# Fusing Phi into K's weights with products of 64 and 60 rows in place of products of 120 rows

## The chip, the core and the metric

The kernel runs on one core of one Trainium2 chip. The metric is the device time of one execution in microseconds (us), the median of several. TensorE (PE in the views) multiplies; its weight loads (PEld) are instructions of their own. VectorE (DVE), ScalarE (ACT) and GpSimd (POOL) do the rest of the arithmetic, and SyncE (SP) issues all the DMAs.

## What is computed

`x` has 2048 tokens of 640 values. It is normalized by row, goes through linear attention with 32 heads of 20 values (A) and beside it through a gated unit of width 1536 (B), and the two results are added to `x`.

```python
def _A_ref(x, wqkv, w_phi, wo):
    B, S, D = x.shape
    H = 32; Dh = D // H
    qkv = (lambda x, *d: x.transpose(*d))((x @ wqkv).reshape(B, S, 3, H, Dh), 2, 0, 3, 1, 4)
    q, k, v = qkv[0], qkv[1], qkv[2]
    pq = jnp.einsum("bhsd,hdf->bhsf", q, w_phi)
    pk = jnp.einsum("bhsd,hdf->bhsf", k, w_phi)
    phi_q = jnp.concatenate([_softmax(pq, axis=-1), _softmax(-pq, axis=-1)], axis=-1)
    phi_k = jnp.concatenate([_softmax(pk, axis=-1), _softmax(-pk, axis=-1)], axis=-1)
    kv = jnp.einsum("bhsf,bhsd->bhfd", phi_k, v)
    z  = jnp.einsum("bhsf->bhf", phi_k)
    num = jnp.einsum("bhqf,bhfd->bhqd", phi_q, kv)
    den = jnp.einsum("bhqf,bhf->bhq", phi_q, z)[..., None] + 1e-6
    o = num / den
    return (lambda x, *d: x.transpose(*d))(o, 0, 2, 1, 3).reshape(B, S, D) @ wo
...
def _B_ref(x, w1, w3, w2):
    gate = jnp.einsum("bsd,df->bsf", x, w1)
    up = jnp.einsum("bsd,df->bsf", x, w3)
    h = _silu(gate) * up
    out = jnp.einsum("bsf,fd->bsd", h, w2)
...
return x + _A_ref(xn, A_wqkv, A_w_phi, A_wo) + _B_ref(xn, B_w1, B_w3, B_w2)
```

Since `pk = xn Wk Phi`, with Phi block-diagonal (a 20x20 block for each head), the kernel forms the 640x640 matrices `Wk Phi` and `Wq Phi` once. This document is about how these small products are made.

## The kernel before

The order of every engine's work is written out by hand (`tc.manual_schedule`, line 156): each engine runs its instructions in the order of the Python text, and semaphores do the rest. SP's queue has the DMAs in that order too.

**The start** (lines 173 to 235 and 756 to 823). The first tiles of `x`, 128 tokens each, and the weights for V are loaded. Until `x` is there, TensorE is given idle products: two of ones (line 225) and 40 products 64 columns wide on a tile of zeros, `warm(2 * WARM, P // 2)` (line 226). Then come the transposes of the first tiles by TensorE (`by_pe`, line 294), whose PSUM results ACT copies (line 301), and the norm's statistics (`ln_stats`, `ln_root`). A one-element copy on POOL (line 775) makes the DMA of `x` tiles 4 and 5 wait for the root of tile 1; the first slices of the gated unit's weights w1 and w3 (`ld_glu1`) stand around it in SP's queue. `warm(4)` (line 759) stands between the first two groups of transposes.

**Fusing Phi.** `ldT` (line 157) loads Wk, and later Wq, transposed by the DMA: slice `c` has 128 columns of the weight from column `AT[c]` on in its 128 partitions. `AT` is 0, 120, ... 480 and 520, so a slice's first 120 rows hold six heads of 20. `wps` holds the rows of `w_phi` that belong to them, and POOL spreads them with a mask of ones and zeros into blocks (`phi_blocks`, line 431): `wphi[:, c]` is a 120x120 block-diagonal piece of Phi. `fuse` (line 437) makes one 128-row piece `d` (of five) of the fused matrix with six products, `c` = 0 to 5, of 120 contraction rows: the transposed weight is the stationary operand (128 columns of it, reloaded for each product) and `wphi[:, c]` moves, 120 columns wide, 40 for the last. Slices 0 to 2 land in one PSUM bank (360 columns), 3 to 5 in another (280). ACT copies the first to `wkphi` or `wqphi`, DVE or ACT the second.

K's five pieces, `FB(0)` to `FB(4)` (line 747), stand at lines 885 to 894: FB(0) and FB(1) together, FB(2) and FB(3) together, FB(4) alone; V's product of a token tile (`V(14)`, and that for tile 15) stands between them. Right behind FB(4) comes the loop over the 16 token tiles (line 901), whose `phi_unit` multiplies a tile by `wkphi` (five row pieces, two products each) and takes the exponentials. Q's five pieces are made inside this loop, in its turns 4 to 8 (line 908), for the loop over Q's tiles behind it. Other small products in the trace: `kv_unit` (line 498, products 61 columns wide) and `r_unit` (line 530, 63 wide).

Of the kernel before, what the change touches and what calls it, by code (L numbers as in the profile page):

```python
# [8 lines left out]
P = 128  # L9
# [3 lines left out]
def kernel(  # L13
# [17 lines left out]
    nc = tc.nc  # L31
    bf = mybir.dt.bfloat16
# [10 lines left out]
    EPS = 1e-5  # L43
    SAFE = 36.0
    BY_ROOT = 6
    WARM = 20
    RAW = 3


# [2 lines left out]
    CH = 6 * 3 * Dh  # L52

    VC = 1 + 3 * Dh

    NF, FR, LH = 6, 120, 6
    AT = [120 * c for c in range(5)] + [D - 120]

    x2 = A_x[0]
    out2 = out[0]  # L60
# [1 line left out]
    one = ctx.enter_context(tc.tile_pool(name="one", bufs=1))  # L62
# [4 lines left out]
    def bank(name, dt=f32):  # L67
        n = 512 if dt == f32 else 1024
        return psum.tile([P, n], dt, name=name, tag="bank")

    def pair(name):
        return psum2.tile([P, 2, 512], f32, name=name, tag="pair")


    xnT = one.tile([P, KD, S], bf, name="xnT")
    wkphi = one.tile([P, KD, D], bf, name="wkphi")
    wqphi = one.tile([P, KD, D], bf, name="wqphi")
    w1 = one.tile([P, KD, F], bf, name="w1")
    w3 = one.tile([P, KD, F], bf, name="w3")
    kvr = one.tile([P, NCH, 3, 21], bf, name="kvr")  # L80
# [64 lines left out]
    def ld(dst, src):  # L145
        nc.sync.dma_start(out=dst, in_=src)
# [4 lines left out]
    def ld_glu(f0, f1):  # L151
        for w, src in ((w1, B_w1), (w3, B_w3)):
            ld(w[:, :, f0:f1], src[:, f0:f1].rearrange("(c p) f -> p c f", p=P))

    wps = one.tile([P, NF, Dh], bf, name="wps")
    with tc.manual_schedule():
        def ldT(dst, i, c):
            a = i * D + AT[c]
            nc.sync.dma_start_transpose(out=dst[:, c], in_=A_wqkv[:, a : a + P])
# [19 lines left out]
        for c in range(2, KD):  # L179
# [7 lines left out]
        eps = one.tile([P, 1], f32, name="eps")  # L187
        nc.gpsimd.memset(eps[:], EPS)

        mask = one.tile([P, LH], bf, name="mask")  # L190
        nc.gpsimd.memset(mask[:], 1.0)
        nc.gpsimd.affine_select(
            out=mask[:], in_=mask[:], pattern=[[-20, LH]], base=0,
            channel_multiplier=1, compare_op=ALU.is_ge, fill=0.0,
        )
        nc.gpsimd.affine_select(
            out=mask[:], in_=mask[:], pattern=[[20, LH]], base=19,
            channel_multiplier=-1, compare_op=ALU.is_ge, fill=0.0,
        )

# [4 lines left out]
            out=own[:], in_=own[:], pattern=[[-64, 2], [-20, 3]], base=0,  # L205
# [3 lines left out]
            out=own[:], in_=own[:], pattern=[[64, 2], [20, 3]], base=19,  # L209
# [5 lines left out]
        idle = bank("idle")  # L215
        nought = one.tile([P, P], bf, name="nought")
        nc.vector.memset(nought[:], 0.0)

        def warm(n, cols=P):
            for _ in range(n):  # L220
                nc.tensor.matmul(idle[:, 0:cols], nought[:], nought[:, 0:cols])  # L221

        lit = nc.const_aps.tensor(1.0, [P, P], bf)
        for _ in range(2):
            nc.tensor.matmul(idle[:, 0:P], lit, lit)
        warm(2 * WARM, P // 2)

        nc.gpsimd.memset(phi[:, :, :, :, 60:64], 0.0)

# [11 lines left out]
        def ln_stats(*ts):  # L241
            made = []
            for t in ts:
                xt = xin[:, (t // 4) % 3, t % 4, :]
                st = work.tile([P, 2, 6], f32, name="st")
                for i in range(2):
                    nc.vector.bn_stats(out=st[:, i, :], in_=xt[:, i * HD : (i + 1) * HD])  # L247
                made.append(st)
            for t, st in zip(ts, made):
                nc.vector.bn_aggr(out=mv[:, t, :], in_=st[:])  # L250
# [43 lines left out]
        def by_pe(dst, t, ps):  # L294
            xt = xin[:, (t // 4) % 3, t % 4, :]
            for c in range(KD):
                nc.tensor.transpose(
                    ps[:, c * P : (c + 1) * P], xt[:, c * P : (c + 1) * P], ident[:]
                )
# [48 lines left out]
        def tile_of(t):  # L348
            return slice(t * P, (t + 1) * P)

        def by_token(cols, w, name, cut, ps=None):

            ps = ps or [bank(name), bank(name)]
            for c in range(KD):
                for i in range(2):
                    a, b = (0, cut) if i == 0 else (cut, D)
                    nc.tensor.matmul(  # L357
                        ps[i][:, 0 : b - a],
                        xnT[:, c, cols],
                        w[:, c, a:b],  # L360
                        start=(c == 0),
                        stop=(c == KD - 1),
                        skip_group_check=True,
                    )
            return ps
# [63 lines left out]
        wphi = one.tile([P, NF, LH, Dh], bf, name="wphi")  # L429

        def phi_blocks():
            nc.gpsimd.tensor_mul(
                out=wphi[0:FR],
                in0=wps[0:FR, :, None, :].to_broadcast([FR, NF, LH, Dh]),
                in1=mask[0:FR, None, :, None].to_broadcast([FR, NF, LH, Dh]),
            )

        def fuse(dst, wT, d, ps, copy=None):

            for c in range(NF):  # L440
                b, i = divmod(c, 3)
                h0 = 4 if c == NF - 1 else 0
                nc.tensor.matmul(  # L443
                    ps[b][:, FR * i : FR * i + Dh * (LH - h0)],
                    wT[0:FR, c, d * P : (d + 1) * P],
                    wphi[0:FR, c, h0:LH],
                    start=(i == 0),
                    stop=(i == 2),
                    skip_group_check=True,
                )  # L450
            nc.scalar.copy(out=dst[:, d, 0:CH], in_=ps[0][:, 0:CH])
            (copy or nc.scalar.copy)(out=dst[:, d, CH:D], in_=ps[1][:, 0 : D - CH])

        def glu_unit(sc, fi, banks=None):

# [243 lines left out]
        def fill(n):  # L699
            for _ in range(n):  # L700
                glu_unit(*glu.pop(0))()
# [38 lines left out]
        def two(name):  # L740
            both = pair(name)
            return both[:, 0], both[:, 1]

        def V(t, ps=None):
            v_unit(vaug[:, t], tile_of(t), ps)

        def FB(d):
            fuse(wkphi, wkT, d, [bank("pf"), bank("pf")] if d % 2 else two("pf"), nc.scalar.copy if d == 4 else nc.vector.tensor_copy)


        def by_dma(t):
# [4 lines left out]

        pst = [bank("pst", bf), bank("pst", bf)]
        by_pe(xrT, 0, pst[0])
        warm(4)
        ln_stats(0)  # L760
        ln_root(0)
        by_pe(xrT, 1, pst[1])
# [71 lines left out]
        ld_tiles(12, 2)  # L834
        ld_tiles(14, 2)
        w_phi = A_w_phi.rearrange("h j f -> (h j) f")
        ld(wps[0:FR, 0:5], w_phi[0 : 5 * FR].rearrange("(c p) f -> p c f", p=FR))
        ld(wps[0:FR, 5], w_phi[D - FR : D])
        stats(8, 2)
        g3 = unit()  # L840
        g2()
# [40 lines left out]
        V(13)  # L882
        g8 = unit()
        g8()
        FB(0)
        FB(1)
        ld_glu(512, F)
        V(14)
        FB(2)
        FB(3)  # L890
        for c in range(NF):
            ldT(wqT, 0, c)
        ps = by_token(tile_of(15), wv, "pv", CH)
# [7 lines left out]
        for i, t in enumerate(turns):  # L901
            phi_unit(t, wkphi, "pk")
            if i > 1:
                kv_unit(turns[i - 2], vaug[:, turns[i - 2]], acc, i == 2, False)
            if i and i not in (2, 3, 6, 7, 14, 15):
                fill(1)
            if 4 <= i < 9:
                fuse(wqphi, wqT, i - 4, [bank("pf"), bank("pf")])
            fill(1)
            if i == 0:  # L910
                nc.sync.dma_start_transpose(out=wvT, in_=A_wqkv[:, 2 * D : 3 * D])
            if 4 <= i < 9:
                column_sum(i - 4)
            if i == 9:
                ld(row[:].rearrange("c p -> p c"), sums[:])
                ld(less_sum, row[:].rearrange("c p -> (c p)").partition_broadcast(P))
            if 11 <= i < 11 + RAW:
                raw_centred(i - 11)
            if i >= 12:
                norm_unit(wkphi, 0, i - 12)  # L920
# [71 lines left out]
    with tc.If(ok == 0) as general:  # L992
# [4 lines left out]
        with tc.For_i(0, NST, 1) as t:  # L997
            cols = bass.ds(t * P, P)
# [4 lines left out]
            for i, half in enumerate(halves):  # L1003
                n = half.shape[1]
                nc.vector.tensor_tensor(out=half, in0=half, in1=acc[:, i, 0:n], op=ALU.add)
        kv_done(halves)
        with tc.For_i(0, NST, 1) as t:
# [5 lines left out]
            h = hT[:, bass.ds(t, 1)].rearrange("p a f s -> p (a f) s")  # L1013
# [33 lines left out]
```

## Time and profile before

| what | value |
|---|---|
| median of 3 runs | 267.82 us (267.74 to 268.05) |
| the profiled execution: its own time | 269.46 us |
| the profiled execution: span from the first to the last instruction | 267.7 us |
| busy share of the span | PE 97%, DVE 72%, PEld 57%, ACT 43%, POOL 34% |

The profile is of one execution. Its views give for each instruction the engine, the line of the kernel, the tile written, the tiles read (`out<-in`), and start and duration. A matmul's row has the array's rows and columns in use (`120*128`) and the operand's shape (partitions x columns). A matmul's duration runs from its start to a modelled end, and matmuls overlap: the pace of a row of matmuls is read from their number and the time from the first start to the next group's start, which the chain of waits gives. A few matmul records are missing from a trace.

### The profile page before, as it was taken

Reading aid. Unit: us, or ns where it says so; the run is one execution under the profiler, and the core shown is the slowest. Engines: PE = TensorE matmul, PEld = TensorE weight load, DVE = VectorE, ACT = ScalarE, POOL = GpSimd, SP = SyncE. Lnnn points to the kernel's source line nnn. Section 1 sums busy time; section 2 is a strip of 40 time slices with the busy share of each in tenths; the row PEclk is TensorE's granted clock in tenths of the full one; section 3 lists DMA queues with packets and bytes.
Section 4 is the critical chain, followed back from the end, with each engine's and each line's share of the span. In section 5 each row is a group of like instructions: output and inputs, shape, how many; then the busy total and the mean of one; then the engine's idle time right before and its main releaser. Section 6 shows DMA issues by size and latency. Waiting matters only on the chain.

```text
span 267.7 us, 5000 instructions
## 1 busy us (share of the span) xinstructions
PE 260.8 (97%) x1840; PEld 152.9 (57%) x1866; DVE 192.9 (72%) x355; ACT 113.8 (43%) x349; POOL 90.7 (34%) x83
## 2 busy tenths in 40 slices
PE   8979999999999999999999999999999999999995
PEld 7756565756556555555555555555555554644573
DVE  5879982488877777799988999999799876215121
ACT  5863445664567754455856664432422240000000
POOL 5022540035544633444364333335533553000000
PEclk9999999999999999999999999999999999999999
DMA  6994966996000000700007945363964979553681
GB/s 194 285 177 114 152 126 124 385 146 125 1 0 2 1 3 2 172 2 0 2 0 196 210 107 120 85 157 85 125 145 111 180 183 176 127 122 66 177 226 55
DMA packets 82828, 31.25 MB, mean 117 GB/s; under 512 B 71279, under 2 KB 81391, under 8 KB 82800
## 3 DMA queue, kind: packets, MB, share of 16 engines
q1 hardware_dynamic: 82800, 30.89, 53.0%
q8 instruction: 16, 0.26, 0.4%
q14 instruction: 12, 0.10, 0.1%
HBM read 11.17 MB, written 2.63 MB: 52 GB/s over the span
## 4 chain that ended last, share of the span: by engine, by line
PE 94%; DMA 3%; issue 1%; ACT 1%; DVE 0%; SPq 0%; POOL 0%
PE up L459 18%; PE gp L459 18%; PE acc L645 15%; PE pq L357 8%; PE pk L357 8%; PE acc L598 7%; PE pv L357 6%; PE acc L650 6%; DMA w<-in_B_w_dram 3%; PE pr L535 2%; PE pkv L500 2%; PE pf L443 1%; PE up L476 1%; PE idle L221 1%; ACT reg_w L301 0%
## 5 line engine op out<-in xcount | busy, mean ns | idle before, releaser
L423 POOL TENSOR_TENSOR phi<-phi,rk 128x1320 bf16<-128x1320 bf16 x32 | 77.2, 2414 | 109.3 <-DVE rk L422 87.7
L459 PEld LDWEIGHTS <-w 128*128 128x128 bf16 x450 | 42.6, 97 | 46.9
L420 DVE TENSOR_REDUCE sk<-phi 128x66 f32<-128x1320 bf16 x32 | 48.8, 1525 | 19.7 <-ACT phi L386 18.4
L459 PE MATMUL up<-xnT,w 128*128 128x512 bf16 x224 | 55.9, 379 | 0.2
L459 PE MATMUL gp<-xnT,w 128*128 128x512 bf16 x207 | 54.4, 378 | 0.8
L357 PEld LDWEIGHTS <-xnT 128*128 128x128 bf16 x450 | 42.8, 98 | 19.2
L386 ACT ACTIVATE phi<-pq 128x360 bf16<-128x360 f32 (+2 forms) x96 | 24.8, 366 | 42.1 <-issue 31.8
L470 ACT ACTIVATE th<-gp 128x512 f32<-128x512 f32 x48 | 29.4, 612 | 28.1 <-PE gp L459 26.8
L645 PE MATMUL acc<-reg_h,reg_v 128*128 128x512 bf16 x180 | 41.3, 379 | 0.0
L490 DVE SCALAR_TENSOR_TENSOR reg_h<-gs,up 128x512 bf16<-128x512 bf16 x48 | 33.0, 687 | 5.4 <-PE pv L357 0.5
L487 DVE SCALAR_TENSOR_TENSOR gs<-th,gp 128x512 bf16<-128x512 f32 x48 | 31.4, 653 | 5.2 <-ACT th L470 5.2
L386 ACT ACTIVATE phi<-pk 128x360 bf16<-128x360 f32 (+2 forms) x96 | 24.9, 370 | 19.4 <-PE pk L357 19.4
L645 PEld LDWEIGHTS <-reg_v 128*128 128x128 bf16 x180 | 17.4, 98 | 19.1
L357 PE MATMUL pk<-wkphi,xnT 128*128 128x360 bf16 (+1 forms) x160 | 24.3, 299 | 0.0
L357 PE MATMUL pq<-wqphi,xnT 128*128 128x360 bf16 (+1 forms) x160 | 24.3, 299 | 0.0
L422 DVE RECIPROCAL rk<-sk 128x66 f32<-128x66 f32 x32 | 18.1, 567 | 3.2
L357 PE MATMUL pv<-reg_w,xnT 128*128 128x360 bf16 (+1 forms) x130 | 18.6, 299 | 0.0
L247 DVE BATCH_NORM_STATS2 st<-reg_h 128x6 f32<-128x320 bf16 x32 | 13.4, 476 | 3.5 <-DMA reg_h<-in_A_x_dram 3.5
L653 DVE TENSOR_TENSOR w<-acc,v_raw 128x512 bf16<-128x512 f32 x10 | 6.6, 670 | 11.6 <-issue 5.8
L607 DVE TENSOR_TENSOR res<-acc,xr 128x320 bf16<-128x320 f32 (+2 forms) x8 | 3.6, 487 | 15.7 <-PE acc L598 10.8
L372 ACT CAST reg_v<-pv 128x360 bf16<-128x360 f32 (+2 forms) x39 | 10.6, 347 | 9.7 <-PE pv L357 9.7
L556 DVE TENSOR_TENSOR o__77<-pr,den 128x360 bf16<-128x360 f32 (+1 forms) x32 | 14.2, 485 | 0.6
(90 smaller groups left out, 210.7 us busy)
## 6 DMA issues: line engine op xcount, KB each, us to landing
w<-in_B_w_dram SPq DMA_DIRECT2D x2, 1280.0 KB, 7.2
reg_v<-in_B_w_dram SPq DMA_DIRECT2D x1, 1920.0 KB, 8.8
out_dram<-w SPq DMA_DIRECT2D x6, 320.0 KB, 2.7
reg_h<-in_A_x_dram SPq DMA_DIRECT2D x5, 320.0 KB, 5.6
w<-in_B_w_dram SPq DMA_DIRECT2D x4, 320.0 KB, 9.3
reg_h<-in_A_x_dram SPq DMA_DIRECT2D x6, 160.0 KB, 2.9
reg_w<-in_A_wqkv_dram SPq DMA_DIRECT2D x5, 160.0 KB, 3.7
reg_w<-in_A_wo_dram SPq DMA_DIRECT2D x1, 800.0 KB, 7.3
```

The source lines that it names most:

```text
L357: nc.tensor.matmul(ps[i][:, 0 : b - a], xnT[:, c, cols], w[:, c, a:b], start=(c == 0), stop=(c == KD - 1), skip_group_check=True,)
L386: nc.scalar.activation(out=dst[:, c0 : c0 + n, g, 0:k], in_=p.rearrange("p (c f) -> p c f", c=n), func=AF.Exp, scale=1.0 - 2.0 * g,)
L420: nc.vector.reduce_sum(out=sk[:], in_=rows, axis=AX.X)
L422: nc.vector.reciprocal(out=rk[:], in_=sk[:])
L423: nc.gpsimd.tensor_mul(out=rows, in0=rows, in1=rk[:, :, :, None].to_broadcast([P, 2 * NCH, 3, Dh]))
L459: nc.tensor.matmul(ps, w[:, c, fi * P : (fi + 1) * P], xnT[:, c, sc * 512 : (sc + 1) * 512], start=(c == 0), stop=(c == KD - 1),)
L470: nc.scalar.activation(out=th[:], in_=gp, func=AF.Tanh, scale=0.5)
L487: nc.vector.scalar_tensor_tensor(out=gs[:], in0=th[:], scalar=1.0, in1=gp, op0=ALU.add, op1=ALU.mult)
L490: nc.vector.scalar_tensor_tensor(out=hT[:, 4 * sc : 4 * sc + 4, fi, :], in0=gs[:].rearrange("p (t s) -> p t s", t=4), scalar=0.5, in1=up.r ...
L598: nc.tensor.matmul(ps[:, 0 : b - a], rows[j][0], rows[j][1][:, a:b], start=(j == 0), stop=(j == len(rows) - 1),)
L645: nc.tensor.matmul(acc4, w2[:, k, cols], hT[:, 4 * g : 4 * g + 4, k, :], start=(k == 0), stop=False,)
L650: nc.tensor.matmul(acc[:], wo[:, k, cols], oTs[g][:, k, :], start=False, stop=(k == KD - 1),)
```

## The change

Three things change together.

1. K's fusion. `AT` becomes 0, 36, 156, ... 516, and a slice's first 124 rows are used. Slice 0 gives heads 0 and 1 in one product over 124 rows, 60 columns wide (20 columns of zeros ahead of the two heads; `wkphi` has 20 columns more in front for them). Each further slice holds six heads in rows 4 to 123: three in rows 4 to 63 and three in rows 64 to 123. Two products are made of it, one over rows 0 to 63 into one PSUM bank and one over rows 64 to 123 into the other, each 60 columns wide. FB(0) and FB(1) are merged, and FB(2) and FB(3): the 124-row products of both pieces come first, then the pairs. ACT's copy takes the six groups of 60 of one bank to every other group of the result, the other copy the five groups of the other bank.
2. Q's fusion keeps one product for a slice, now over 124 rows: 60 columns for the first and 120 for the five others. POOL's spreading of Phi and the load of `wps` are split differently (slice 0, slices 1 to 5).
3. The 40 idle products 64 columns wide become 8 that are 256 wide (64 columns, each read four times) and 8 that are 64 wide.

```diff
-    NF, FR, LH = 6, 120, 6
-    AT = [120 * c for c in range(5)] + [D - 120]
+    NF, FR, LH = 6, 124, 6
+    AT = [0] + [2 * Dh - 4 + LH * Dh * c for c in range(NF - 1)]
...
-    wkphi = one.tile([P, KD, D], bf, name="wkphi")
-    wqphi = one.tile([P, KD, D], bf, name="wqphi")
+    wkpad = one.tile([P, KD, Dh + D], bf, name="wkphi")
+    wqpad = one.tile([P, KD, Dh + D], bf, name="wqphi")
+    wkphi, wqphi = wkpad[:, :, Dh:], wqpad[:, :, Dh:]
...
-        def warm(n, cols=P):
+        def warm(n, cols, times=1):
             for _ in range(n):
-                nc.tensor.matmul(idle[:, 0:cols], nought[:], nought[:, 0:cols])
+                nc.tensor.matmul(
+                    idle[:, 0 : cols * times], nought[:],
+                    nought[:, 0:cols, None].to_broadcast([P, cols, times]),
+                )
...
-        warm(2 * WARM, P // 2)
+        warm(8, P // 2, 4)
+        warm(8, P // 2)
...
+        def fuse_rows(dst, wT, parts):
+
+            def product(d, ps, c, b, r0, r1, h):
+                i = c - b
+                nc.tensor.matmul(
+                    ps[b][:, 60 * i : 60 * i + 60],
+                    wT[r0:r1, c, d * P : (d + 1) * P],
+                    wphi[r0:r1, c, h : h + 3],
+                    start=(i == 0),
+                    stop=(c == NF - 1),
+                    skip_group_check=True,
+                )
+
+            for d, ps, _ in parts:
+                product(d, ps, 0, 0, 0, FR, 0)
+            for d, ps, copy in parts:
+                for c in range(1, NF):
+                    product(d, ps, c, 1, 0, 64, 0)
+                    product(d, ps, c, 0, 64, FR, 3)
+                groups = dst[:, d].rearrange("p (c k) -> p c k", k=60)
+                for b, n, op in ((0, 6, nc.scalar.copy), (1, 5, copy)):
+                    op(
+                        out=groups[:, b::2],
+                        in_=ps[b][:, 0 : 60 * n].rearrange("p (c k) -> p c k", k=60),
+                    )
...
-                h0 = 4 if c == NF - 1 else 0
+                a = 120 * i - (60 if 0 < c < 3 else 0)
                 nc.tensor.matmul(
-                    ps[b][:, FR * i : FR * i + Dh * (LH - h0)],
+                    ps[b][:, a : a + (120 if c else 60)],
                     wT[0:FR, c, d * P : (d + 1) * P],
-                    wphi[0:FR, c, h0:LH],
+                    wphi[0:FR, c, 0 : 6 if c else 3],
...
-        warm(4)
+        warm(4, P)
...
-        FB(0)
-        FB(1)
+        FB(0, 1)
         ld_glu(512, F)
         V(14)
-        FB(2)
-        FB(3)
+        FB(2, 3)
```

More of the change, by code (lines that the diff above doesn't have):

```diff
@@ L45 @@
     BY_ROOT = 6
-    WARM = 20
     RAW = 3
@@ L188 @@
         nc.gpsimd.memset(eps[:], EPS)
-        mask = one.tile([P, LH], bf, name="mask")
+        mask = one.tile([P, 2, LH], bf, name="mask")
         nc.gpsimd.memset(mask[:], 1.0)
         nc.gpsimd.affine_select(
-            out=mask[:], in_=mask[:], pattern=[[-20, LH]], base=0,
+            out=mask[:], in_=mask[:], pattern=[[-24, 2], [-20, LH]], base=20,
             channel_multiplier=1, compare_op=ALU.is_ge, fill=0.0,
@@ L196 @@
         nc.gpsimd.affine_select(
-            out=mask[:], in_=mask[:], pattern=[[20, LH]], base=19,
+            out=mask[:], in_=mask[:], pattern=[[24, 2], [20, LH]], base=-1,
             channel_multiplier=-1, compare_op=ALU.is_ge, fill=0.0,
@@ L431, in phi_blocks, with fuse @@
         def phi_blocks():
[L432 to L438, printed above, removed]
+            for k, a, b in ((0, 0, 1), (1, 1, NF)):
+                nc.gpsimd.tensor_mul(
+                    out=wphi[0:FR, a:b],
+                    in0=wps[0:FR, a:b, None, :].to_broadcast([FR, b - a, LH, Dh]),
+                    in1=mask[0:FR, k : k + 1, :, None].to_broadcast([FR, b - a, LH, Dh]),
+                )
[21 more added lines that the diff above has]
+                        in_=ps[b][:, 0 : 60 * n].rearrange("p (c k) -> p c k", k=60),
+                    )
+        def fuse(dst, wT, d, ps):
             for c in range(NF):
                 b, i = divmod(c, 3)
-                h0 = 4 if c == NF - 1 else 0
+                a = 120 * i - (60 if 0 < c < 3 else 0)
                 nc.tensor.matmul(
-                    ps[b][:, FR * i : FR * i + Dh * (LH - h0)],
+                    ps[b][:, a : a + (120 if c else 60)],
                     wT[0:FR, c, d * P : (d + 1) * P],
-                    wphi[0:FR, c, h0:LH],
+                    wphi[0:FR, c, 0 : 6 if c else 3],
                     start=(i == 0),
@@ L450, in fuse @@
                 )
-            nc.scalar.copy(out=dst[:, d, 0:CH], in_=ps[0][:, 0:CH])
-            (copy or nc.scalar.copy)(out=dst[:, d, CH:D], in_=ps[1][:, 0 : D - CH])
+            nc.scalar.copy(out=dst[:, d, 0:300], in_=ps[0][:, 0:300])
+            nc.scalar.copy(out=dst[:, d, 300:], in_=ps[1][:, 0:360])
         def glu_unit(sc, fi, banks=None):
@@ L745, in V, with FB @@
             v_unit(vaug[:, t], tile_of(t), ps)
-        def FB(d):
-            fuse(wkphi, wkT, d, [bank("pf"), bank("pf")] if d % 2 else two("pf"), nc.scalar.copy if d == 4 else nc.vector.tensor_copy)
+        def FB(*ds):
+            fuse_rows(wkpad, wkT, [
+                (d, [bank("pf"), bank("pf")] if d % 2 else two("pf"), nc.scalar.copy if d == 4 else nc.vector.tensor_copy)
+                for d in ds
+            ])
         def by_dma(t):
@@ L836 @@
         w_phi = A_w_phi.rearrange("h j f -> (h j) f")
-        ld(wps[0:FR, 0:5], w_phi[0 : 5 * FR].rearrange("(c p) f -> p c f", p=FR))
-        ld(wps[0:FR, 5], w_phi[D - FR : D])
+        ld(wps[0:FR, 0], w_phi[0:FR])
+        ld(wps[0:FR, 1:NF], bass.AP(
+            tensor=w_phi.tensor, offset=w_phi.offset + AT[1] * Dh,
+            ap=[[Dh, FR], [LH * Dh * Dh, NF - 1], [1, Dh]],
+        ))
         stats(8, 2)
@@ L907 @@
             if 4 <= i < 9:
-                fuse(wqphi, wqT, i - 4, [bank("pf"), bank("pf")])
+                fuse(wqpad, wqT, i - 4, [bank("pf"), bank("pf")])
             fill(1)
```

## The prediction

> **What bounds the kernel now.** The page comes first, then a table by stage with TensorE alone.
>
> ```profile
> PE 260.8 (97%) x1840; PEld 152.9 (57%) x1866; DVE 192.9 (72%) x355; ACT 113.8 (43%) x349; POOL 90.7 (34%) x83
> ```
>
> ```profile
> core 0: us, PE busy (x), PEclk, DMA share, GB/s
> 15.20:47.00 31.80, 31.63 (x197) 1.00 0.77 140
> 47.00:52.00 5.00, 5.00 (x57) 1.00 1.04 394
> 52.00:94.00 42.00, 41.68 (x312) 1.00 0.31 58
> 94.00:255.00 161.00, 160.10 (x1078) 1.00 0.52 107
> ```
>
> From 15.2 to 255 us TensorE never rests: the four stretches are busy for 238.41 of 239.80 us, 99.4%. So in this part TensorE sets the time, and the price of an edit is the TensorE time that it adds or removes; a faster ACT or DVE would bring nothing. All of the fusion lies there. The chain of waits gives the pace of K's five pieces and of what stands around them (columns: start, length, work).
>
> ```profile
> 46.27 1.08 PE up L459 x5
> 47.35 0.57 PE pf L443 x12
> 47.93 1.36 PE pv L357 x10
> 49.29 0.57 PE pf L443 x12
> 49.86 1.36 PE pv L357 x10
> 51.23 0.28 PE pf L443 x6
> 51.51 1.36 PE pk L357 x10
> ```
>
> The fusion is 1.42 us for K (0.57 + 0.57 + 0.28), 47 ns a product, with nothing lost before or behind it: all pieces of this chain join. The matmul durations of the groups by shape are longer than that pace because they overlap:
>
> ```profile
> L443 PE MATMUL pf<-wphi,reg_w 120*128 120x120 bf16 x50 | 4.0, 215 | 0.0
> L443 PE MATMUL pf<-wphi,reg_w 120*128 120x40 bf16 x10 | 1.8, 183 | 0.0
> L221 PE MATMUL idle<-nought 128*128 128x64 bf16 x40 | 2.3, 242 | 0.0
> ```
>
> Eighty columns more cost 32 ns, 0.4 ns a column, so a 40-wide product of 183 ns is 16 ns of columns and 167 ns of way through the array, which the next product normally shares.
>
> The first 15 us have another bound:
>
> ```profile
> 1.21 2.16 PE idle L221 x40
> 3.36 0.55 PE pst L297 x5
> ...
> 5.91 0.19 POOL reg_h L775
> ...
> 6.11 0.37 SPq L146
> ...
> 6.53 8.64 DMA w<-in_B_w_dram
> ...
> 15.21 1.26 PE up L476 x10
> ```
>
> TensorE waits there for the first slice of the gated unit's weights, whose DMA is issued behind the marker on POOL, and the idle products head that chain. They take 54 ns each (2.16 us / 40), twice 64 columns at 0.4 ns: the array runs at half pace there, though the view's clock column says 1.00.
>
> **K's products.** Thirty products go, 640 columns a piece. In their place stand five 60-wide products over 124 rows and 25 pairs of 60-wide ones. The nearest rows are narrow products with their own weight loads.
>
> ```profile
> 82.35 0.33 PE pkv L500 x11
> ```
>
> Eleven products, ten of them 61 wide, take 0.33 us: 30 ns each, though 61 columns would be 24 ns. The trace has no product of under 120 rows, so whether two halves of the rows run beside each other is not in it. The bounds for a pair are 30 ns (the two overlap entirely) and 60 ns (one after the other). I take 30: the halves use different rows of the array and of the operands, and land in different banks, so nothing in the code ties the second to the first. Then K's fusion is 5 x 30 + 25 x 30 ns = 0.90 us in place of 1.42: **-0.52 us**. With 60 ns it is 1.65 us, +0.23.
>
> **Going into split rows and back.** This is the price that the trace doesn't show. Merging leaves three groups, each between products over the whole array, so six changes. Zero is the lower bound, since a wait can't be negative; going from 120 to 128 rows costs nothing now, as the joined chain shows. If the array had to run empty, the next product would lose the 167 ns that it otherwise shares, so 0 to 1.0 us for six. The nearest row in between is a weight load that can't be fetched ahead:
>
> ```profile
> L443 PEld LDWEIGHTS <-reg_w x60: 95/97/100, 47.0 to 93.2; 120*128 120x128 bf16 x60
> ```
>
> A load takes 97 ns. Some 30 ns of it is paid by every narrow product anyway: of a fusion's 0.28 us five 120-wide products take about 50 ns each (48 ns of columns) and leave 30 for the 40-wide one, whose columns are 16. That leaves 0.07 us; with a little for the array I take 0.08 us a change, **+0.48 us**. The Trainium skill, page TensorEngine Tiling (Array Packing), Key Properties, states the rule that speaks against this change: changing the tiling mode, not merely the tile, drains TensorE. No run here shows it so far; by the rule the sum would take the upper bound, 1.0 us, and the kernel would be slower by about half a microsecond.
>
> **Q's products.** Their number stays; the first is 60 wide in place of 120 and the last 120 in place of 40, so 20 columns more, 8 ns a piece at 0.4 ns:
>
> ```profile
> 72.25 0.28 PE pf L443 x6
> ```
>
> Five pieces make +0.04 us at most and, since a 60-wide product has the same 30 ns floor as a 40-wide one nearly has, 0.01 at least. I take **+0.02 us**. They go from 120 to 124 rows and stay unsplit.
>
> **The copies.** ACT and DVE copy 360 and 300 columns where it was 360 and 280. Only FB(4)'s copies have TensorE close behind them:
>
> ```profile
> 51.36 0.31 PE L357 MATMUL pk<-wkphi,xnT 128*128 128x360 bf16 x1
> ```
>
> ```profile
> 51.56 0.46 ACT L451 CAST wkphi<-pf 128x360 bf16<-128x360 f32 x1 [0.81 <-PE pf L443]
> 51.92 0.40 ACT L452 CAST wkphi<-pf 128x280 bf16<-128x280 f32 x1
> ```
>
> The last row piece of `wkphi` is needed by the ninth product of that tile, 8/10 of 1.36 us behind its first: 51.36 + 1.09 = 52.45. The second copy ends at 52.32. Until now that ninth product needed only the first copy's columns, up to 360; now the columns of both copies interleave, and it needs both. Twenty columns more are about 0.02 us ((0.46 - 0.40) / 80 x 20), so 0.11 us of cover is left. If it were gone, each 0.1 us late would cost 0.1 us; a change back to whole rows delays the loop and widens it. Price 0. V's last copies stand behind them on ACT and begin as much later; no product nearby reads what they write. The merged groups ask for the second piece's banks some 0.25 us sooner, and DVE's and ACT's readers of those banks are three pairs of tiles back.
>
> **POOL and the DMAs.**
>
> ```profile
> 33.20 1.39 POOL L432 TENSOR_TENSOR wphi<-wps,mask 120x720 bf16<-120x720 bf16 x1
> ```
>
> ```profile
> 24.71 1.01 SPq L146 DMA_DIRECT2D wps<-in_A_w_phi_dram  x2
> ...
> 38.23 3.89 SPq L159 DMA_TRANSPOSE reg_w<-in_A_wqkv_dram  x3
> ```
>
> POOL's one spreading becomes two, 120 and 600 values a row. Even at twice 1.39 us it would end at 36.0, 11 us before FB(0) at 47.35; without that cover FB(0) would begin as much later. Behind it on POOL stands the statistics work of tiles 14 and 15. The two loads of `wps` stay two, in the same place, and the transposed slices keep their number and order; only start addresses move. Price 0; cover gone, a slice that lands late would hold FB(0), but the last K slice is issued by 42.1, five microseconds ahead.
>
> **The idle products.** 8 x 256 + 8 x 64 = 2560 columns, as 40 x 64 were. At half pace that is the same 2.16 us, price 0. They end about when `x` comes:
>
> ```profile
> 3.11 0.89 DVE L247 BATCH_NORM_STATS2 st<-reg_h 128x6 f32<-128x320 bf16 x2 [2.12 <-DMA reg_h<-in_A_x_dram]
> 3.13 0.50 PEld L297 LDWEIGHTS <-reg_h 128*128 128x128 bf16 x5
> 3.17 0.72 PE L297 MATMUL pst<-ident,reg_h 128*128 128x128 bf16 x5
> ```
>
> The load for the first transpose starts 0.02 us behind the arrival, the transpose at 3.17; ending sooner would win 0.06 us at most. Being late costs more, below.
>
> **Sum.** -0.52 + 0.48 + 0.02 = -0.02 us against the profiled execution's span of 267.7. That execution's own time was 269.46, 1.64 above the median of the runs, 267.82, and I apply the difference to the median: **267.8 us**. About 0.2%, 0.54 us, is what a measurement of this kernel can tell from no change.
>
> **Rivals.**
>
> *The changes cost nothing* (267.3). If split and whole rows follow each other as 120 and 128 rows do now, -0.50 is left; with pairs at the 28 ns of a 40-wide product, -0.56, 267.26. For it: the seamless chain; against it: a weight load would have to be fetched ahead across the change.
>
> *The halves don't overlap* (slower, 268.5). The weight loads decide: there is one for each half, 55 narrow products, 30 ns each as in the row of eleven, 1.65 us, and the six changes 0.48: +0.73. It is slower than before by the 0.54 once a pair takes over 52 ns: 0.15 + 25 x 0.052 - 1.42 + 0.50 = 0.53. For it: 61 columns already need 30 ns in place of 24, so something other than columns paces narrow products. The Trainium skill, page TensorE: Matmul & The Clock Gate, says that starts never come closer than about 25 ns however small the product; if that holds across row halves, an estimate from it is 50 ns a pair and +0.48 us, while its part on packing small matmuls has products in other rows start some 4 ns apart. No run here shows which.
>
> *The array runs empty at each change* (268.3). 6 x 0.167 = 1.0, with overlapping pairs -0.50 + 1.0 = +0.5; without, +1.25, 269.1.
>
> *The wide idle products are slower* (269.5). Each column is read four times in a row, an operand form that no row here shows. At twice the price the eight wide ones end 1.7 us later; the transposes, the copies and root on ACT behind them, the marker and the DMA of the chain above follow, and TensorE's start at 15.21 with them. Against it: at half pace the operand is read slowly anyway.
>
> *No split happens* (268.1): both halves run as whole-array products, no overlap and no change: +0.25.
>
> **How the numbers follow.** Forecast 0.32; free changes 0.26, of which 0.18 lies beyond 0.2%; no overlap 0.20; empty array 0.12, 0.08 of it beyond 0.2%; slow idle products 0.05; no split 0.05. So faster 0.18; same 0.32 + 0.08 + 0.04 + 0.05 = 0.49; slower 0.20 + 0.08 + 0.05 = 0.33. The forecast's own range is 267.55 to 268.05 (0.04 to 0.12 us a change). The range 267.15 to 268.9 takes in the cases down to a pair of 26 ns with free changes and up to the lost overlap with changes of 0.14 us; it leaves out the empty array without overlap and the slow idle products, about 0.12.
>
> **What would show it.** In the chain, the first two groups of K's products at 0.36 us plus two changes, 0.52 together, in place of 0.57, and the third at 0.34 in place of 0.28. In the instructions in order of time, the starts within a pair under 10 ns apart would show overlap, 25 to 30 ns its lack; a gap between the last whole-row product and the first split one shows the change's price. The first transpose should start at 3.17 and TensorE's work at 15.21, as now. The prediction is wrong if K's three groups together are under 1.0 or over 1.9 us, or if anything outside them moves TensorE by 0.2 us.

## The result, and the profile after

The changed kernel takes 269.0 us (median of 6, 268.64 to 269.75) against 267.78 for the kernel before on the same chip: 1.0048 of it, 95% interval 1.0034 to 1.0063, some 1.2 to 1.3 us slower. The forecast was no change, with a range that ended at 268.9.

The first reading misleads. The span of the changed kernel's profiled execution is *shorter* than the one that the prediction was read from, 267.4 against 267.7 us, though its time is longer than the median before. The profile before belonged to an execution of 269.46 us; its start had waited 1.9 us for the gated unit's weights (the piece of 8.64 us in the chain quoted in the prediction), which is not typical. So the kernel before was profiled again, beside the experiments: 267.60 us, span 265.9. From here on "before" is that profile.

First, what the prediction was mostly about. The chain of waits of the kernel before, in its new profile, from K's fusion to the end of the first tile's product with the fused matrix:

```profile
45.52 0.57 PE pf L443 x12
46.09 1.36 PE pv L357 x10
47.45 0.57 PE pf L443 x12
48.02 1.36 PE pv L357 x10
49.39 0.28 PE pf L443 x6
49.67 1.36 PE pk L357 x10
51.03 0.22 PE gp L459
...
263.02 0.42 DVE res L607
```

The same stretch of the changed kernel:

```profile
46.72 0.44 PE pf L447 x22
47.16 1.46 PE pv L361 x10
48.62 0.44 PE pf L447 x22
49.06 1.47 PE pv L361 x10
50.53 0.27 PE pf L447 x11
50.80 1.47 PE pk L361 x10
52.27 0.43 PE gp L490 x2
...
264.48 0.42 DVE res L638
```

The fusion's pieces are shorter (0.44 for 0.57), and the product behind each is 0.10 to 0.11 longer: the way back to whole rows is counted there. From the first fusion product to the end of the first `pk` it is 5.51 us before and 5.55 after. So the fusion came out even, as forecast. But the changed kernel arrives at it 1.2 us later, and from the end of that first `pk` to the last sum it takes 212.21 us in place of 211.99. The loss is in two places where the prediction saw none.

The bigger one shows in the chain, and in the row of V's products of the changed kernel (the row's last column is idle time and its releaser; in the kernel before, TensorE has no wait in this stretch):

```profile
33.48 0.61 DVE reg_h L293 x2
34.09 2.66 DMA xnT<-reg_h
36.75 0.05 issue
36.80 4.25 PE pv L361 x30
...
L361 PE MATMUL pv<-reg_w,xnT 128*128 128x360 bf16 (+1 forms) x130 | 18.8, 299 | 0.9 <-DMA xnT<-reg_h 0.9
```

TensorE waits until 36.80 for the transposed `x` of tile 10, whose transpose was issued at 34.09. SP's queue in order of time says why, first before:

```profile
22.36 1.04 SPq L146 DMA_DIRECT2D reg_h<-in_A_x_dram  x2
23.45 1.00 SPq L146 DMA_DIRECT2D wps<-in_A_w_phi_dram  x2
24.50 3.54 SPq L159 DMA_TRANSPOSE reg_w<-in_A_wqkv_dram  x2
28.14 2.54 SPq L752 DMA_TRANSPOSE xnT<-reg_h  x2
30.74 1.26 SPq L159 DMA_TRANSPOSE reg_w<-in_A_wqkv_dram  x1
32.09 3.87 SPq L752 DMA_TRANSPOSE xnT<-reg_h  x3
```

and after:

```profile
22.44 1.04 SPq L146 DMA_DIRECT2D reg_h<-in_A_x_dram  x2
23.54 0.75 SPq L146 DMA_DIRECT2D wps<-in_A_w_phi_dram  x2
24.34 5.71 SPq L159 DMA_TRANSPOSE reg_w<-in_A_wqkv_dram  x2
30.15 2.54 SPq L786 DMA_TRANSPOSE xnT<-reg_h  x2
32.74 1.26 SPq L159 DMA_TRANSPOSE reg_w<-in_A_wqkv_dram  x1
34.09 2.55 SPq L786 DMA_TRANSPOSE xnT<-reg_h  x2
```

Up to the loads of Phi's rows (`wps`) the two queues run alike. Then the two transposes of K's first slices hold SP for 5.71 us in place of 3.54, the first alone 4.40, and all that is behind them starts 2.0 us later: tiles 8 and 9, a slice, tile 10 at 34.09 in place of 32.09. TensorE waits 1.1 us of it: the products of tiles 8 and 9 start at 32.97 and take 1.36 us each, so those of tile 10 were due at 35.69 (the 0.9 in the row above counts only from the modelled end of the product in front). So there had been 0.9 us of slack. The other 0.1 us of the 1.2 lies ahead of 33 us, where one execution differs from another by more than that: the first product with w3 starts between 13.0 and 13.7 us in the thirteen traces without a late start. What stands right ahead of the slow transpose are the two loads of `wps`, now on 124 partitions.

### The profile page after: what moved, and what is told of

Its sections match the earlier page's. It is cut to its first block, busy times and chain, and to the rows that moved or that the text cites. A ratio compares the mean times of both kernels' runs of the same rounds, so it can differ in the third digit from the quotient of the medians.

```text
span 267.4 us, 5028 instructions
## 1 busy us (share of the span) xinstructions
PE 262.3 (98%) x1867; PEld 151.6 (57%) x1867; DVE 193.2 (72%) x355; ACT 113.8 (43%) x349; POOL 90.7 (34%) x84
## 4 chain that ended last, share of the span: by engine, by line
PE 91%; DVE 3%; DMA 2%; POOL 1%; SPq 1%; issue 1%; DVEq 0%
PE gp L490 17%; PE up L490 17%; PE acc L676 15%; PE pk L361 8%; PE pq L361 8%; PE acc L629 7%; PE acc L681 6%; PE pv L361 4%; PE pr L566 2%; PE pkv L531 2%; DMA reg_h<-in_A_x_dram 1%; DVE reg_h L521 1%; DMA xnT<-reg_h 1%; PE pv L312 1%; PE gp L507 1%; PE up L507 1%
## 5 line engine op out<-in xcount | busy, mean ns | idle before, releaser
L490 PE MATMUL gp<-xnT,w 128*128 128x512 bf16 x225 | 55.9, 378 | 0.0
```

The costliest lines, as they stand in the source:

```text
L490: nc.tensor.matmul(ps, w[:, c, fi * P : (fi + 1) * P], xnT[:, c, sc * 512 : (sc + 1) * 512], start=(c == 0), stop=(c == KD - 1),)
```

## The experiments

All times are medians in us, and the ratio to the kernel before on the same chip with its 95% interval stands behind them.

**The kernel before again.**

> The kernel before, unchanged, profiled beside the others on one chip. The profile that the prediction was read from belongs to an execution of 269.46 us, 1.64 above the median. If that execution was a late start and no more, this one shows a span near 266.1 us, TensorE past the gated unit's first weight slices near 13.6 us in place of 15.2, and K's fusion starting some 1.6 us earlier, near 45.6. If the profile before was typical, the span is 267.7 again and the start 15.2.

267.67, 0.9996 (0.9987 to 1.0004); the profiled execution 267.60, span 265.9. The late start was that one execution's.

**Phi's rows on 120 partitions.**

```diff
-        ld(wps[0:FR, 0], w_phi[0:FR])
-        ld(wps[0:FR, 1:NF], bass.AP(
-            tensor=w_phi.tensor, offset=w_phi.offset + AT[1] * Dh,
-            ap=[[Dh, FR], [LH * Dh * Dh, NF - 1], [1, Dh]],
-        ))
+        ld(wps[0:120, 0], w_phi[0:120])
+        ld(wps[4:FR, 1:NF], w_phi[2 * Dh : D].rearrange("(c p) f -> p c f", p=120))
...
+        nc.gpsimd.memset(wps[:], 0.0)
```

> The changed kernel, with Phi's rows loaded into 120 partitions (0 to 119 for the first slice, 4 to 123 for the others, the rest zeroed once by POOL) in place of 124. Theory A (the load into 124 partitions runs on few DMA engines, holds up SP's queue for 3 us, and so the transposes of x): 267.6 to 267.9 us, some 1.2 below the changed kernel; the issue of the first transposed slice of K's weight takes 1.2 us in place of 4.4; no wait of TensorE for x at 36 us. Theory B (the split products or the idle products cost it): 269.0 as before. Theory C (the shifted slices' own transposes are slow): 269.0, the issue still 4.4 us.

268.14, 1.0012 (1.0003 to 1.0021): 0.36% below the changed kernel, some 0.96 us, though not quite down to the forecast. SP's queue:

```profile
23.33 0.91 SPq L146 DMA_DIRECT2D wps<-in_A_w_phi_dram  x2
24.29 2.91 SPq L159 DMA_TRANSPOSE reg_w<-in_A_wqkv_dram  x2
27.30 3.52 SPq L787 DMA_TRANSPOSE xnT<-reg_h  x2
```

The transposes of the slices take 2.91 us again, with the same shifted start columns, and no wait of TensorE is left: theory A, not B or C. About 0.3 us over the kernel before remain to be explained.

**124 partitions in the kernel before, for the large load.**

```diff
-        ld(wps[0:FR, 0:5], w_phi[0 : 5 * FR].rearrange("(c p) f -> p c f", p=FR))
         ld(wps[0:FR, 5], w_phi[D - FR : D])
+        ld(wps[0:124, 0:5], bass.AP(
+            tensor=w_phi.tensor, offset=w_phi.offset,
+            ap=[[Dh, 124], [FR * Dh, 5], [1, Dh]],
+        ))
```

> The kernel before, but Phi's first five slices are loaded into 124 partitions (4 rows of each are not used), and behind the small load in place of ahead of it, as in the changed kernel. Nothing else changes. Theory A: 268.5 to 269.0 us, the first transposed slice's issue 3 us longer. Theories B and C: 267.8.

267.62, 0.9998 (0.9990 to 1.0007): a miss. The mechanism shows without the loss:

```profile
24.07 4.38 SPq L159 DMA_TRANSPOSE reg_w<-in_A_wqkv_dram  x2
28.55 2.55 SPq L752 DMA_TRANSPOSE xnT<-reg_h  x2
```

The first slice alone is held for 3.07 us, but the transposes of `x` start only 0.4 us later than before (28.55, 28.14), within the 0.9 us of slack.

**The two loads in the other order.** The changed kernel:

```diff
-        ld(wps[0:FR, 0], w_phi[0:FR])
         ld(wps[0:FR, 1:NF], bass.AP(
...
         ))
+        ld(wps[0:FR, 0], w_phi[0:FR])
```

> The changed kernel with its two loads of Phi in the other order, the large one first, both still into 124 partitions. Theory A: the number of DMA engines decides, 268.6 to 269.2 us. A rival to it, that the order decides (the large load right ahead of the transposes): 267.7 to 268.0.

268.96, 1.0039 (1.0027 to 1.0051). The order doesn't decide.

```profile
23.45 2.99 SPq L146 DMA_DIRECT2D wps<-in_A_w_phi_dram  x2
26.48 3.74 SPq L159 DMA_TRANSPOSE reg_w<-in_A_wqkv_dram  x2
```

Here the second load of `wps` is itself held (2.99 us for the two in place of 0.75), so it isn't only a transpose that waits behind such a load. Tile 10's transpose is issued at 34.27, as late as in the changed kernel.

**Aligned starts.** With 120 partitions:

```diff
-    wkpad = one.tile([P, KD, Dh + D], bf, name="wkphi")
-    wqpad = one.tile([P, KD, Dh + D], bf, name="wqphi")
-    wkphi, wqphi = wkpad[:, :, Dh:], wqpad[:, :, Dh:]
+    wkrow = one.tile([P, KD, 32 + D], bf, name="wkphi")
+    wqrow = one.tile([P, KD, 32 + D], bf, name="wqphi")
+    wkpad, wqpad = wkrow[:, :, 32 - Dh :], wqrow[:, :, 32 - Dh :]
+    wkphi, wqphi = wkrow[:, :, 32:], wqrow[:, :, 32:]
```

> The changed kernel with Phi's rows in 120 partitions, and with 12 columns more in front of the fused matrices, so that the part that moves through TensorE starts at byte 64 of a row of 1344 in place of byte 40 of a row of 1320. Theory D (the shifted start costs 4.5 ns in each 280-wide product that begins 8 bytes off a multiple of 16, three of ten products of a tile): those products go from 123 back to 119 ns; the time from the first product with K's fused matrix to the last product of all goes from 213.71 to 213.47 us, and the kernel is 0.24 us below the one with 120 partitions: level with the kernel before within 0.1%. Rival (that time is longer because of Q's 20 columns more a piece, or the 124 rows): it stays at 213.7.

267.80, 1.0004 (0.9995 to 1.0013). In its chain the fusion begins, the first `pk` ends and the last sum begins at

```profile
45.80 0.44 PE pf L449 x22
...
51.34 0.22 PE gp L492
...
263.35 0.42 DVE res L640
```

that is 212.01 us from the end of that `pk` to the last sum, against 211.99 before and 212.21 in the changed kernel: theory D. One trace of each is enough here, because this part hardly varies: from the first product behind that `pk` to the last product of all it is 211.84 to 211.87 us in the nine traces with aligned matrices and 212.03 to 212.06 in the five with shifted ones. The starts of the single products in the trace show where it sat. Mean time from the start of a product with `wkphi` to the next start, ns, by row piece (16 tiles each; "bytes" is the start within a row of the tile, modulo 16):

```
                                     piece 0   1      2      3      4
before           wkphi, 280 wide     118.9   119.1  119.5  118.9  119.5   bytes 0 0 0 0 0
120 partitions   wkphi, 280 wide     123.4   118.4  123.4  118.4  123.4   bytes 8 0 8 0 8
                 wkphi, 360 wide     152.9   151.6  151.9  151.6  151.8   bytes 8 0 8 0 8
120, aligned     wkphi, 280 wide     119.3   119.1  119.2  119.2  119.1   bytes 0 0 0 0 0
before, padded   wkphi, 280 wide     123.2   118.5  123.4  118.2  123.6   bytes 8 0 8 0 8
```

With `wqphi` it is alike (122.5, 118.2, 123.2, 118.2, 123.2 with 120 partitions). Three products of 4.5 ns in each of the 31 tiles that are left would make 0.42 us, and the stretch grows by 0.2 only. Part of the difference is in the same traces: with the shift, the other products follow each other some 0.5 to 0.9 ns sooner than before (118.4 for 119.1, 151.6 for 152.5), so that a tile's ten products take 8 to 10 ns more in all. The rest, under 0.1 us, is not accounted for.

**The same shift put into the kernel before.**

```diff
-    wkphi = one.tile([P, KD, D], bf, name="wkphi")
-    wqphi = one.tile([P, KD, D], bf, name="wqphi")
+    wkpad = one.tile([P, KD, Dh + D], bf, name="wkphi")
+    wqpad = one.tile([P, KD, Dh + D], bf, name="wqphi")
+    wkphi, wqphi = wkpad[:, :, Dh:], wqpad[:, :, Dh:]
```

> The kernel before with 20 unused columns in front of both fused matrices, as the changed kernel has them; nothing else changes. Theory D: the 280-wide products of the first, third and fifth row piece take 123 in place of 119 ns, the time from the first product with K's fused matrix to the last product goes from 213.47 to about 213.7, and the kernel takes 0.2 to 0.3 us more than before. Rival: no change.

267.94, 1.0004 (0.9995 to 1.0013): too little for the clock to tell. The trace tells it: 123 in place of 119 ns in the same three pieces, and

```profile
51.16 0.22 PE gp L460
...
263.35 0.43 DVE res L608
```

212.19 us, 0.20 more than before. So the shift alone makes the 0.2 us.

**Two loads on 124 partitions in the kernel before.** `wpx` is a tile that nobody reads.

```diff
+        ld(wps[0:FR, 5], w_phi[D - FR : D])
         by_dma(6)
...
-        ld(wps[0:FR, 0:5], w_phi[0 : 5 * FR].rearrange("(c p) f -> p c f", p=FR))
-        ld(wps[0:FR, 5], w_phi[D - FR : D])
+        ld(wpx[0:124], w_phi[0:124])
+        ld(wps[0:124, 0:5], bass.AP(
+            tensor=w_phi.tensor, offset=w_phi.offset,
+            ap=[[Dh, 124], [FR * Dh, 5], [1, Dh]],
+        ))
```

> The kernel before, with both loads of Phi ahead of the transposes on 124 partitions: one of 124 single rows (into a tile that nobody reads), then the large one; the sixth slice's own load stands earlier in the queue, where SP waits anyway. Theory A, sharpened (descriptors a DMA engine decide, 31 + 155 on four engines, not the order and not the slices' start): the first transposed slice's issue takes over 4 us, the transposes of x start some 1.5 to 2 us later than in the kernel before, TensorE waits 0.7 to 1.3 us for tile 10, and the kernel takes 268.5 to 269.1. Rival (the shifted slices or the changed kernel's own order of work are needed for the wait): 267.7.

268.32, 1.0021 (1.0013 to 1.0030), 0.56 us over the kernel before: the kernel before gets slower by its loads' partitions alone, but less than expected, and less than the 0.96 us that the changed kernel got back. The profiled execution, 267.73, was the shortest of the twelve; there the first slice is held for 3.1 us and TensorE doesn't wait. So no trace shows this variant's wait.

**The idle products alone.** The kernel before, with the changed `warm`:

```diff
-        warm(2 * WARM, P // 2)
+        warm(8, P // 2, 4)
+        warm(8, P // 2)
```

> The kernel before with the 16 idle products of the changed one alone. Theory: no difference, 267.6 to 267.8; the wide ones take 213 ns each (256 columns at half pace), and the first transpose starts at 3.17 as before. Rival (four reads of one column are slow): the first transpose starts later and the kernel takes up to 1.7 us more.

267.79, 0.9999 (0.9989 to 1.0008). TensorE in order of time, this variant and then the kernel before:

```profile
1.05 2.31 PE L221 MATMUL idle<-nought 128*128 128x256 bf16 x16
3.17 0.72 PE L301 MATMUL pst<-ident,reg_h 128*128 128x128 bf16 x5
```

```profile
1.05 2.31 PE L221 MATMUL idle<-nought 128*128 128x64 bf16 x40
3.17 0.72 PE L297 MATMUL pst<-ident,reg_h 128*128 128x128 bf16 x5
```

Reading each column four times costs nothing at this pace, and the first transpose starts at the same instant.

**No split.** Aligned, 120 partitions:

```diff
-        def fuse(dst, wT, d, ps):
+        def fuse(dst, wT, d, ps, copy=nc.scalar.copy):
...
-            nc.scalar.copy(out=dst[:, d, 300:], in_=ps[1][:, 0:360])
+            copy(out=dst[:, d, 300:], in_=ps[1][:, 0:360])
...
-            fuse_rows(wkpad, wkT, [
-                (d, [bank("pf"), bank("pf")] if d % 2 else two("pf"), nc.scalar.copy if d == 4 else nc.vector.tensor_copy)
-                for d in ds
-            ])
+            for d in ds:
+                fuse(wkpad, wkT, d, [bank("pf"), bank("pf")] if d % 2 else two("pf"), nc.scalar.copy if d == 4 else nc.vector.tensor_copy)
```

> The changed kernel with Phi's rows in 120 partitions and aligned starts, and with K's pieces made like Q's: six whole-row products of 124 rows, 60 and five times 120 columns, no split and no pairs. If the split is worth nothing here, the time from the first fusion product of K to the first product with the fused matrix is 4.16 to 4.19 us, against 4.173 with the pairs, and the kernel is within 0.1% of the one with them. If the pairs gave something, it is longer by their 0.5 us.

267.72, 0.9998 (0.9989 to 1.0007).

```profile
45.80 0.58 PE pf L476 x12
46.38 1.36 PE pv L363 x10
...
51.33 0.86 PE gp L492 x4
```

5.53 us for the stretch, against 5.54 with pairs: the split is worth nothing here.

**Five groups in place of three.** Aligned, 120 partitions:

```diff
-        FB(0, 1)
+        FB(0)
+        FB(1)
...
-        FB(2, 3)
+        FB(2)
+        FB(3)
```

> The changed kernel with Phi's rows in 120 partitions and aligned starts, and with the five pieces of K each in a group of its own: the same 55 products, but ten changes between whole and split rows in place of six. With a pair at 27 ns and a change at 0.09 to 0.10 us, as read from the starts in the changed kernel's trace, each lone piece takes 0.369 us and the fusion 1.85 in place of 1.44: the stretch from its first product to the first product with the fused matrix grows from 4.17 to 4.58 us, and the kernel is 0.4 us slower. With changes that cost nothing, it stays at 4.17.

268.06, 1.0015 (1.0005 to 1.0024).

```profile
45.69 0.65 PE pf L449 x22
46.34 1.46 PE pv L363 x10
...
51.65 0.43 PE gp L492 x2
```

5.96 us in place of 5.54: four more changes, 0.42 us, 0.105 each. The medians (268.06, and 267.80 with three groups) differ by 0.26 us; the trace is the sharper of the two.

**The loads of Phi earlier.** The changed kernel, 124 partitions and shift included:

```diff
+        ld(wps[0:FR, 0], w_phi[0:FR])
+        ld(wps[0:FR, 1:NF], bass.AP(
...
         by_dma(6)
         by_dma(7)
...
-        ld(wps[0:FR, 0], w_phi[0:FR])
-        ld(wps[0:FR, 1:NF], bass.AP(
```

> The changed kernel as it is, with 124 partitions and the shifted starts, but its two loads of Phi stand earlier in SP's queue, ahead of the transpose of tile 6, where SP waits for DVE. Theory A (the loads hurt because the transposes of later tiles queue behind them): the first transposed slice's issue falls from 4.4 us to below 2, no wait for tile 10, and the kernel falls to 267.9 to 268.3, where the one with 120 partitions is. If the place doesn't matter: 269.

268.08, 1.0009 (0.9998 to 1.0021): 0.39% below the changed kernel, some 1.0 us, by the place of two DMAs alone.

```profile
18.20 0.73 SPq L146 DMA_DIRECT2D wps<-in_A_w_phi_dram  x2
19.70 2.75 SPq L786 DMA_TRANSPOSE xnT<-reg_h  x2
...
23.64 2.48 SPq L159 DMA_TRANSPOSE reg_w<-in_A_wqkv_dram  x2
```

**127 partitions.** The kernel before with the small load first, and the large one:

```diff
-        ld(wps[0:FR, 0:5], w_phi[0 : 5 * FR].rearrange("(c p) f -> p c f", p=FR))
+        ld(wps[0:127, 0:5], bass.AP(
+            tensor=w_phi.tensor, offset=w_phi.offset,
+            ap=[[Dh, 127], [FR * Dh, 5], [1, Dh]],
+        ))
```

> The kernel before, with the small load of Phi first and the large one on 127 partitions, a prime number, in place of 120; three rows more than with 124. Theory A as a rule on engines (the load runs on as many DMA engines, up to 16, as divide its partitions evenly): 635 runs of 40 bytes go through one engine, 7 us at 11 ns each; the first transposed slice's issue takes 6 to 9 us, the transposes of x start 4 to 6 us later, and the kernel takes 271 to 273. If only the number of rows mattered, it is as with 124: 267.6.

270.43, 1.0090 (1.0070 to 1.0110), 2.7 us slower (0.6 less than the expected least).

```profile
24.39 7.33 SPq L159 DMA_TRANSPOSE reg_w<-in_A_wqkv_dram  x2
31.82 2.63 SPq L752 DMA_TRANSPOSE xnT<-reg_h  x2
```

Three rows a slice more than with 124, and the transposes of `x` start 3.3 us later still (31.82, 28.55). The DMA packets of 40 bytes, counted by their starts in half microseconds from 25.5 on, show the pace of the loads:

```
before,          120 partitions: 237 360  79  44
124 partitions, changed kernel:    4  72 201 216 199  52
127 partitions, kernel before:    58 132  71  79  71  71  71  70  71  61
```

With 127 it is a steady 71 in half a microsecond, with 124 some 200, and with 120 up to 360. (The first two bins of the last row also hold the 120 packets of the small load.) In the three cases the first slice's transpose is released at 25.8, 28.7 and 30.4, when these packets begin (120) or are over (124, 127). This fits a rule in the Trainium skill, page DMA: Bandwidth & Descriptors, section "Why a DMA increments its semaphore by 16 and not by 1": a DMA runs on the largest number of engines up to 16 that divides the slowest dimension of both its access patterns, which gives 15 for 120 partitions, 4 for 124 and 1 for 127. The traces agree in the order of the three. They don't tell the engines apart, but the pace bears out the 4 against the 1: in the kernel with earlier loads, also on 124 partitions, no other packet starts between 20.0 and 21.0, and there 274 and then 284 of these packets start in half a microsecond, which is four times 71. With 120 partitions the packets are over before a steady pace shows, so the 15 is not shown.

## Why the prediction was wrong, point by point

**K's products: right.** A pair was put at 30 ns, the halves side by side. In the changed kernel the second product of a pair starts 3 ns behind the first and pairs follow each other by 27 ns (46.751, 46.754, 46.778, 46.781 us). The rival in which the halves don't overlap falls, and with it, between row halves, the 25 ns that the page TensorE: Matmul & The Clock Gate of the Trainium skill gives as the least between starts.

**Going into split rows and back: right in size.** 0.08 us was taken. The last whole-row product and the first split one start 0.121 us apart in place of 0.031 (46.591, 46.712), and the way back is 0.119 in place of 0.027: 0.09 each. The kernel with five groups gives 0.105. The next start behind a change is another 0.01 us late (0.039 in place of 0.027 going in, 0.163 in place of 0.152 coming back), which brings the two figures together at 0.10. The rule of the Trainium skill, page TensorEngine Tiling (Array Packing), says that TensorE drains at such a change. The trace agrees in that a pause is there, at some 60% of the 0.167 us that was the upper bound; whether the array runs empty in it is not shown. The reason that the prediction gave for its 0.08 isn't borne out: it took the length of a weight load that isn't fetched ahead, while the trace shows a pause ahead of the load. The load of the first split product starts 0.117 us behind the last whole-row product (46.591, 46.708), where the weight loads of the whole-row products start 1 to 3 ns behind the product in front, and the product starts 4 ns behind its load. The near-zero sum is luck in part: pairs were 3 ns cheaper than taken, some 0.07 us for 25, and changes 0.02 dearer, 0.12 for six, two errors that partly cancel. Pairs win, changes lose, and the sum of the two was put at -0.04 us; the stretch measures +0.04 against the kernel before (5.55, 5.51) and +0.01 against whole-row products of the new slices.

**Q's products, the copies, the idle products: right.** No wait on the copies appears, and Q's pieces take 0.29 to 0.30 us each, 0.28 to 0.29 before. Aligned and on 120 partitions, the changed kernel is level with the one before.

**POOL and the DMAs: this step failed.** It said of the loads of Phi that they "stay two, in the same place", and priced them at 0. The number of partitions had no term: with 124 in place of 120 the packets of the load start at 200 or so in half a microsecond in place of up to 360, and the next issue on SP takes 4.40 us. And the victim was named wrongly: not a slice that lands late for FB(0), but the transposes of `x` that stand behind the slices in SP's queue, which had 0.9 us of slack. Putting the loads on 120 partitions gave back 0.36%, some 0.96 us, and putting them elsewhere 0.39%. It is the last of the prediction's own signs of being wrong that came true: something outside K's groups moved TensorE by more than 0.2 us.

**A term that was missing.** That "only start addresses move" was said of the slices; that the fused matrices themselves now start at byte 40 of a longer row was in the diff and not in the sum. The prediction put it at nothing; it costs 0.2 us, by the same stretch with the shift, without it, and before (212.21, 212.01 and 211.99). With the 0.96 us of the wait it makes 1.2 of the 1.2 to 1.3 us.

**The base.** The prediction's chain of the start, the idle products ahead of a DMA that ends at 15.17, was one execution's. It also hid how little slack the transposes of `x` have: the first product with w3 started at 15.21 there and at 13.38 in the new profile, so TensorE reached tile 10 some 1.8 us later than it usually does. That TensorE sets the time there was true of the kernel before, with less to spare than that profile could show.

**What stays open.** In the changed kernel's profiled execution the first slice is held until 28.7, in the kernel before with both loads on 124 partitions until 27.2. The packets of the loads of `x` ahead of them end at 26.9 in the one and 25.9 in the other, which goes with it; whether the shifted rows of Phi or the chance of one execution make that difference was not tried. With it stays open why the kernel before, with both loads on 124 partitions, lost only 0.56 us where the changed kernel got back 0.96, and why SP is held for about as long as such packets run.

## What to carry to other kernels

When a slice's partition count changes, look at every DMA that fills it, and at what stands behind that DMA in its queue: loads of 744 runs of 40 bytes held back work that they had nothing to do with. Splitting small products over row halves pays only in long runs: about 0.2 us for going in and out against 25 ns saved for each pair of 60-wide products in place of one 120-wide. And before a sum is made on a profile, hold its time against the median: in a profile whose start comes late, work behind the start has more slack than it usually has.

## What the runs showed that was not expected

A product of 280 columns whose operand starts 8 bytes off a multiple of 16 takes 4.5 ns more (123.4 against 118.9), and one of 360 columns takes no more (151.8 to 152.9 against 152.3 to 152.6 before). The 280-wide product is always the second of its row piece, so width and place were not told apart, and no reason was found.

A load of short runs on 124 or 127 partitions holds up the issue of the next DMA on SP, not only its own landing: 4.40 us with 124 in the changed kernel and 6.02 with 127, for an issue that takes 1.2 to 1.8 in the traces with 120 partitions.
